# New engine orders for a blocked attention kernel, with two first products split by columns and a last part in two

## The chip, the cores and the metric

The kernel runs on one core of a Trainium2 chip. The metric is the device time of one execution in microseconds (us). Most executions of a kernel agree within 0.3%.

## The reference

One layer of multi-head attention with a cached K and V: B = 8 batches, SQ = 112 queries, D = 640 model width, H = 32 heads of DH = 192, SK = 512 keys. All tensors are bf16.

```
q = (x @ wq).reshape(B, Sq, H, Dh).transpose(0, 2, 1, 3)
scores = einsum("bhqd,bhkd->bhqk", q, k_cache) * (Dh ** -0.5)
p = softmax(scores, axis=-1)
o = einsum("bhqk,bhkd->bhqd", p, v_cache)
out = o.transpose(0, 2, 1, 3).reshape(B, Sq, H * Dh) @ wo
```

## The kernel before

**Tiles and stages.** The 32 heads are taken in four rounds of eight. A round has two groups (batches 0 to 3, 4 to 7), so there are eight groups g, and 64 steps n: a step is one batch and half a round, four heads. An operation below is named as in the kernel's lists: a kind, then its numbers.

- ("XT", c): five transposes on PE of 128 rows of x (L656); ("evX", c) copies them from PSUM into xT_sb (the copy helper, L146 on ACT, L147 on DVE).
- ("Q", g, lp, c): a tile of q for group g, pair of heads lp and 128 of its 384 columns c, five matmuls of 128x448 (L721); ("evQ", ...) copies it into qr, and ("qc", n) on POOL, or DVE, brings the second parts of step n's heads together in qh (L762, L763).
- ("KT", i, p): 24 transposes of K for the few K tiles that are loaded as they lie (L673); most K tiles are transposed by the DMA that loads them (("K", i), L158). A K tile serves two steps, 2i and 2i+1.
- ("Sm", n, j) and ("St", n, j): the scores of step n (L774). ("smax", n, k) on DVE takes the maximum and copies the scores to s_sb (L831), ("exp", n, k) on ACT (L836), ("rc", n, j) the reciprocal of the sums (L848), ("norm", n, k) the scaling of p on DVE (L840).
- ("PT", n): 32 transposes of p on PE (L875) with two copies ("evPT", n, t); for steps 57 to 61 instead ("TD", n), a transposing DMA (L859).
- ("PVt", n), ("PVm", n, t): p @ v (L907, L919), copied by ("evPV", n).
- ("O", g, m, half): o @ wo for block m of 128 output columns (L941); ("oacc", g, m) adds it up on DVE (L955, L956). For the last group the part of batch 6 is ("O6", ...) with ("oacc6", ...) (L974, L984), and that of batch 7 ("OL", s, part) with ("oaccL", part) (L998, L1007, L1011). ("OF", b) transposes the sum of batch b back (L1023), ("oout", b) copies it into xT_sb, and ("OUT", b) stores it (L646).

**What sets the order.** Nothing is scheduled while the kernel runs. Five lists written out by hand, ORDER_PE, ORDER_ACT, ORDER_DVE, ORDER_POOL and ORDER_SP, give each engine its operations in order; a copy or small operation runs on the engine in whose list it stands. BANKS gives each PSUM tile one of eight banks; a tile waits until the copy that reads the tile before it in its bank is done. The class Plan numbers the semaphores from the lists, and each engine waits for an operation's inputs just before it issues it, so an engine that waits holds all that stands behind in its list.

**Loads.** All transfers stand on SP, in order. A load waits for its place: K i for the last St of step 2(i−4)+1, which frees the slot; a V half (L167) for the p @ v of the step three tiles before; and each load waits for the landing of an earlier one, so that about 0.95 tile sizes are under way (AHEAD, L1107). The TD of a step waits for its norm operations. SP being in order, a held load holds all later ones, the OUT transfers too.

**Buffers that couple steps.** s_sb has three places, so a smax waits for the exp three before it. The exp operations of step n wait until p of step n − 2 is transposed (its PT, or the landing of its TD), as p_sb is used anew.

**Head and tail.** PE begins with 18 matmuls on zeros (idle, L690), until x has landed; the zeros are set by DVE (L1142). In the tail, batch 7's last products have two parts: part 0 has the blocks 0, 1 and 4, part 1 the blocks 2 and 3. Part 0 is summed by two DVE operations (L1007 for the blocks 0 and 1, L1011 for 4), part 1 by one; ("OF", 7) needs both.

## Time and profile before

| what | value |
|---|---|
| three runs | 434.97, 433.34, 434.41 us; median 434.41 |
| the profiled execution | 434.01 us, of which 432.2 span |
| instructions in the span | 16330 |
| DMA over the span | 122.05 MB moved, mean 282 GB/s |
| granted TensorE clock | 1.00 |

The span is what the profile covers, from the first instruction to the last; the 1.8 us around it are the start and end of the execution. In a timeline row stand the start in us, the length, the engine (PE the matmuls, PEld its weight loads, SPq the issuing of DMAs), the line of the kernel, the operation, output<-input by name, shapes and count; in brackets the idle time before it and what ended that. Names of tiles are those of the place in memory: places are used anew, so K or p can stand under accT, wo_sb or wq_sb. In the rows of the chain of waits stand the start, the length and the work that the end of the execution hung on. A row of groups has the busy time, the mean length in ns, and the idle time before.

### The profile page before, as it was taken

To read this page: it belongs to the slowest core of one execution; us is meant where nothing else is said; L and a number is where in the kernel's file an instruction comes from. 1 tells how busy PE (TensorE), PEld (TensorE's weight loads), DVE (VectorE), ACT (ScalarE), POOL (GpSimd) and SP (SyncE) were. 2 spreads that over 40 slices of the span, in tenths; PEclk is the share of its full clock that TensorE was granted. 3 is DMA by queue.
4 is the path that set the end of the run, shared out by engine and by line. 5 is a ranking of instruction groups with operands and counts; after the bars stand their busy time and mean duration, and the time that the engine had idled before them with its cause. 6 is when DMAs were issued, how large, how long until landed. Compare 5 with 4: busy or idle time off the path is not lost.

```text
span 432.2 us, 16330 instructions
## 1 busy us (share of the span) xinstructions
PE 419.0 (97%) x6805; PEld 289.5 (67%) x6805; DVE 345.6 (80%) x1087; ACT 335.9 (78%) x734; POOL 88.7 (21%) x124
## 2 busy tenths in 40 slices
PE   7999997999999999999999999999999999999986
PEld 4556665676766667677766666766667667666886
DVE  2689887889788888888798997869888679987871
ACT  3489998988868686889777858978778787766763
POOL 0102222122212222222122212222222120212100
PEclk9999999999999999999999999999999999999999
DMA  8999999999999999999999999999999999999772
GB/s 273 372 334 366 346 289 238 330 331 187 238 355 239 215 342 372 321 255 353 269 235 345 277 238 331 369 333 225 236 274 250 216 289 360 314 224 256 197 216 84
DMA packets 218923, 122.05 MB, mean 282 GB/s; under 512 B 165216, under 2 KB 218848, under 8 KB 218848
## 3 DMA queue, kind: packets, MB, share of 16 engines
q1 hardware_dynamic: 218848, 120.99, 107.5%
q8 instruction: 54, 0.88, 0.9%
q14 instruction: 21, 0.17, 0.1%
HBM read 78.22 MB, written 1.15 MB: 184 GB/s over the span
## 4 chain that ended last, share of the span: by engine, by line
PE 84%; DMA 7%; DVE 6%; ACT 1%; issue 1%; SPq 0%; DVEq 0%; ACTq 0%
PE ps L721 20%; PE ps L774 18%; PE ps L941 17%; PE ps L919 12%; PE ps L907 7%; PE ps L875 7%; DMA wq_sb<-p_sb 3%; DVE s_sb L831 3%; PE ps L673 2%; DVE p_sb L840 2%; DMA vt<-in_v_cache_dram 2%; DMA accT<-in_k_cache_dram 1%; DMA kt<-in_x_dram 1%; PE ps L974 1%; ACT p_sb L836 1%
## 5 line engine op out<-in xcount | busy, mean ns | idle before, releaser
L836 ACT ACTIVATE p_sb<-s_sb,nmx 112x512 bf16<-112x512 f32 x256 | 182.8, 718 | 34.0 <-DVE s_sb L831 28.5
L831 DVE TENSOR_SCALAR_CACHE_REDUCE s_sb<-ps 112x512 f32<-112x512 f32 x256 | 169.3, 683 | 30.5 <-PE ps L774 22.1
L762 POOL COPY qh<-qr 64x672 bf16<-64x672 bf16 x59 | 44.0, 746 | 309.1 <-PE ps L774 266.0
L721 PE MATMUL ps<-xT_sb,wq_sb 128*128 128x448 bf16 x480 | 101.5, 353 | 2.4 <-DVE kt L147 1.6
L774 PE MATMUL ps<-kt,qr 128*128 128x256 bf16 (+1 forms) x512 | 95.3, 272 | 0.9 <-DVE s_sb L831 0.7
L941 PE MATMUL ps<-oT_sb,wo_sb 128*128 128x448 bf16 (+1 forms) x480 | 91.4, 341 | 0.0
L840 DVE TENSOR_SCALAR p_sb<-p_sb,rinv 112x512 bf16<-112x512 bf16 x256 | 88.1, 373 | 0.8
L774 PE MATMUL ps<-kt,qh 128*128 128x256 bf16 (+1 forms) x512 | 87.8, 272 | 0.0
L941 PEld LDWEIGHTS ps<-oT_sb,wo_sb 128*128 128x128 bf16 x480 | 44.7, 98 | 36.0 <-issue 0.4
L721 PEld LDWEIGHTS ps<-xT_sb,wq_sb 128*128 128x128 bf16 x480 | 42.6, 98 | 39.0 <-issue 3.5
L146 ACT ACTIVATE oT_sb<-ps 128x672 bf16<-128x672 f32 x64 | 46.5, 726 | 24.8 <-PE ps L919 24.3
L146 ACT ACTIVATE pT_sb<-ps 128x1024 bf16<-128x1024 bf16 (+1 forms) x61 | 55.9, 923 | 10.7 <-PE ps L875 10.7
L774 PEld LDWEIGHTS ps<-kt,qr 128*128 128x128 bf16 (+1 forms) x512 | 44.1, 96 | 22.1 <-issue 12.9
L919 PE MATMUL ps<-pT_sb,vt 128*128 128x112 bf16 x944 | 55.2, 213 | 0.0
L919 PEld LDWEIGHTS ps<-pT_sb,vt 128*128 128x128 bf16 x944 | 47.5, 98 | 4.0
L836 ACT ACTIVATION_READ_ACCUMULATOR p_sb<-s_sb,nmx 112x1 f32 x256 | 49.6, 194 | 0.0
L774 PEld LDWEIGHTS ps<-kt,qh 128*128 128x128 bf16 (+1 forms) x512 | 44.1, 96 | 6.0
L763 POOL COPY qh<-qr 64x672 bf16<-64x672 bf16 x59 | 44.0, 745 | 2.5
L146 ACT ACTIVATE qr<-ps 128x448 bf16<-128x448 f32 x58 | 31.2, 541 | 13.0 <-PE ps L721 12.9
L147 DVE COPY pT_sb<-ps 128x768 bf16<-128x768 bf16 (+1 forms) x57 | 34.5, 607 | 6.9 <-PE ps L875 6.8
L875 PE MATMUL ps<-ident,p_sb 64*128 64x64 bf16 (+1 forms) x1888 | 37.1, 185 | 1.5 <-issue 0.6
L875 PEld LDWEIGHTS ps<-ident,p_sb 64*128 64x128 bf16 (+1 forms) x1888 | 33.4, 94 | 7.1 <-issue 3.1
(58 smaller groups left out, 269.0 us busy)
## 6 DMA issues: line engine op xcount, KB each, us to landing
vt<-in_v_cache_dram SPq DMA_DIRECT2D x64, 768.0 KB, 6.7
wo_sb<-in_wo_dram SPq DMA_DIRECT2D x8, 960.0 KB, 7.6
wq_sb<-in_wq_dram SPq DMA_DIRECT2D x7, 960.0 KB, 7.5
wo_sb<-in_k_cache_dram SPq DMA_DIRECT2D x6, 768.0 KB, 7.3
accT<-in_k_cache_dram SPq DMA_DIRECT2D x4, 768.0 KB, 6.4
vt<-in_k_cache_dram SPq DMA_DIRECT2D x2, 768.0 KB, 8.2
kt<-in_k_cache_dram SPq DMA_DIRECT2D x2, 768.0 KB, 6.9
out_dram<-xT_sb SPq DMA_DIRECT2D x8, 140.0 KB, 2.2
```

The costliest lines, as they stand in the source:

```text
L146: return e.activation(dst, src, ACTF.Copy)
L147: return e.tensor_copy(dst, src)
L721: mm = e.matmul(ps[:, bank, 0:SG], w, v, start=(dc == 0), stop=(dc == DC - 1))
L762: e.tensor_copy(dst[64:128, :, 0:3, :], src[0:64])
L763: return e.tensor_copy(dst[0:64, :, 1:4, :], src[64:128])
L774: return e.matmul(ps[:, 2 * j + odd, hs], q, ktb[j][lo:hi, :, blk, h * 128:(h + 1) * 128], start=first, stop=last, skip_group_check=True)
L831: return e.tensor_scalar(s_sb[:, a, :].rearrange("p (e c) -> p e c", e=2), ps[0:SQ, 2 * j:2 * j + 2, h * 256:(h + 1) * 256], -scale, None, ...
L836: return e.activation(p_sb[:, k, :], s_sb[:, a, :], ACTF.Exp, bias=nmx[:, k:k + 1], scale=-1.0, accum_out=rsum[:, k:k + 1])
L840: return e.tensor_scalar(p_sb[:, k, :], p_sb[:, k, :], rinv[:, k:k + 1], None, op0=ALU.mult)
L875: ends.append(e.transpose(psb[:, bank + t, i * w:(i + 1) * w], p_sb[lo:hi, (4 * n + k) % 8, q * 128:(q + 1) * 128], ident[lo:hi, lo:hi]))
L919: mm = e.matmul(ps[:, b0 + j, 2 * h * SQ:(2 * h + 1) * SQ], vtb[:, h0 + 2 * j + h, d0:d0 + 128], pT(j, h, q), start=(q == 0), stop=(q == 3))
L941: mm = e.matmul(ps[:, bank_of["O", g, m], 0:nc_], wo_sb[:, k, m * 128:(m + 1) * 128], oT_sb[:, g % 2, k, 0:nc_], start=(k == 0), stop=(k = ...
```

## The change

ORDER_PE, ORDER_ACT, ORDER_DVE, ORDER_POOL and BANKS are written anew. ORDER_SP stays as it is. PE's list goes from 736 to 739 operations, ACT's from 476 to 463 and DVE's from 819 to 833: 74 copies go from ACT to DVE, 58 from DVE to ACT, and four operations are new. Beside the lists:

- The two first products ("Q", 0, 1, 1) and ("Q", 0, 1, 0) are split by columns: a new operation ("Qa", ...) computes the columns 0 to 256, which need the first two copies of x alone, and "Q" the other 192.
- The two last parts hold the blocks 0, 1, 2 and 3, 4. Part 0 is summed by one DVE operation of three blocks, and the final transposes, the copy and only then the store of batch 7 are in two parts as well, ("OF", 7, part) and ("oout", 7, part). The copies of batch 6 and of part 1 of batch 7 go to DVE.
- The matmuls on zeros at the start are 8 of 512 columns instead of 18 of 256.

```diff
+    FIRST = ((0, 1, 1), (0, 1, 0))
+    XA = 256
...
-        zeros = k3_flat[:, 4 * D:4 * D + 256]
+        zeros = k3_flat[:, 4 * D:4 * D + 512]
...
         ORDER_PE = [
-            ('XT', 0), ('XT', 1), ('XT', 3), ('XT', 2), ('Q', 0, 1, 1), ('Q', 0, 0, 0), ('Q', 0, 0, 1), ('Q', 0, 1, 0),
+            ('XT', 0), ('XT', 1), ('XT', 3), ('XT', 2), ('Qa', 0, 1, 1), ('Qa', 0, 1, 0), ('Q', 0, 1, 1), ('Q', 0, 1, 0),
...
-            ('PVt', 7), ('PVm', 7, 0), ('PVm', 7, 1), ('Sm', 11, 0), ('Sm', 11, 1), ('St', 11, 0), ('St', 11, 1), ('PT', 9),
+            ('PVt', 7), ('PVm', 7, 0), ('PVm', 7, 1), ('Sm', 11, 0), ('Sm', 11, 1), ('PT', 9), ('Q', 2, 3, 2),
+            ('St', 11, 0), ('St', 11, 1), ('PVt', 8), ('PVt', 9), ('PVm', 9, 0), ('PVm', 9, 1), ('PVm', 8, 0),
...
-            add("SP", ("OUT", b), [("oout", b)], emit, f"mOUT{b % DC}", 16)
+            add("SP", ("OUT", b), [("oout", b)] if b < B - 1 else [("oout", b, 0), ("oout", b, 1)], emit, f"mOUT{b % DC}", 16)
...
-                mm = e.matmul(ps[:, 5, 0:256], zeros[:, 0:128], zeros, start=True, stop=True)
+                mm = e.matmul(ps[:, 5, :], zeros[:, 0:128], zeros, start=True, stop=True)
...
-            def emit(e):
+            def emit(e, c0, c1):
                 for dc in range(DC):
                     w, v = q_tile(g, lp, c, dc, 0, 128)
-                    mm = e.matmul(ps[:, bank, 0:SG], w, v, start=(dc == 0), stop=(dc == DC - 1))
+                    mm = e.matmul(ps[:, bank, c0:c1], w, v[:, c0:c1], start=(dc == 0), stop=(dc == DC - 1))
                 return mm
-            add("PE", ("Q", g, lp, c), q_need(g, lp), emit)
+            if (g, lp, c) in FIRST:
+                add("PE", ("Qa", g, lp, c), [wq_piece[0, lp], ("evX", 0), ("evX", 1)], lambda e: emit(e, 0, XA))
+            add("PE", ("Q", g, lp, c), q_need(g, lp), lambda e: emit(e, XA if (g, lp, c) in FIRST else 0, SG))
...
-        LAST = {0: (7, 0), 1: (7, 1), 4: (7, 2), 2: (6, 0), 3: (6, 1)}
+        LAST = {0: (7, 0), 1: (7, 1), 2: (7, 2), 3: (6, 0), 4: (6, 1)}
+        ENDS = [(0, 1, 2), (3, 4)]
...
-            blocks = (0, 1, 4) if part == 0 else (2, 3)
...
+                m0, n = ENDS[part][0], len(ENDS[part])
+                return e.tensor_tensor(oF[:, 1, m0:m0 + n, 3 * SQ:SG, 0],
+                                       ps[:, 7 - part, 0:n * SQ].rearrange("p (c s) -> p c s", c=n),
+                                       accT[:, 1, m0:m0 + n, 3 * SQ:SG], op=ALU.add)
...
+        def o_final(b, *part):
+            bank = bank_of["OF", b, *part]
+            blocks = ENDS[part[0]] if part else tuple(range(DC))
+            cols = slice(blocks[0] * 128, blocks[-1] * 128 + 128)
...
+            need = ([("oaccL", *part)] if part else [("oacc6", g) for g in range(3)] if b == B - 2 else
...
-            idle(e, 18)
+            idle(e, 8)
```

**PE at its start.** The rows give the line, the operation, output<-input, the shape that is streamed, and the count. In the kernel before, PE runs the matmuls on zeros, the transposes of x, four whole products and the first K transposes:

```order
L690 MATMUL ps<-kt 128x256 x18
L656 MATMUL ps<-ident,kt 128x128 x20
L721 MATMUL ps<-xT_sb,wq_sb 128x448 x20
L673 MATMUL ps<-ident,vt 128x64 x48
L721 MATMUL ps<-xT_sb,wq_sb 128x448 x5
```

In the changed kernel (lines are two further on) the same place reads:

```order
L692 MATMUL ps<-kt 128x512 x8
L658 MATMUL ps<-ident,kt 128x128 x20
L723 MATMUL ps<-xT_sb,wq_sb 128x256 x10
L723 MATMUL ps<-xT_sb,wq_sb 128x192 x10
L723 MATMUL ps<-xT_sb,wq_sb 128x448 x10
L675 MATMUL ps<-ident,vt 128x64 x48
L723 MATMUL ps<-xT_sb,wq_sb 128x448 x10
L658 MATMUL ps<-ident,accT 128x128 x15
```

Two of the four products are now ten matmuls of 256 and ten of 192 columns, and the remaining transposes of x stand together.

**DVE at the softmax of step 59.** In the kernel before, DVE has three maxima of step 59, two sums of output blocks (L956), the fourth maximum, then reciprocals and scalings of step 59 among maxima of step 60:

```order
L831 TENSOR_SCALAR s_sb,nmx<-ps 112x512 x3
L956 TENSOR_TENSOR accT<-ps,accT 128x448 x2
L831 TENSOR_SCALAR s_sb,nmx<-ps 112x512
L848 RECIPROCAL rinv<-rsum 112x2
L840 TENSOR_SCALAR p_sb<-p_sb,rinv 112x512
L831 TENSOR_SCALAR s_sb,nmx<-ps 112x512
L848 RECIPROCAL rinv<-rsum 112x2
L831 TENSOR_SCALAR s_sb,nmx<-ps 112x512
L840 TENSOR_SCALAR p_sb<-p_sb,rinv 112x512 x3
```

In the changed kernel (lines four further on):

```order
L835 TENSOR_SCALAR s_sb,nmx<-ps 112x512 x4
L852 RECIPROCAL rinv<-rsum 112x2
L960 TENSOR_TENSOR accT<-ps,accT 128x448
L844 TENSOR_SCALAR p_sb<-p_sb,rinv 112x512
L960 TENSOR_TENSOR accT<-ps,accT 128x448
L852 RECIPROCAL rinv<-rsum 112x2
L844 TENSOR_SCALAR p_sb<-p_sb,rinv 112x512 x2
L835 TENSOR_SCALAR s_sb,nmx<-ps 112x512 x2
L844 TENSOR_SCALAR p_sb<-p_sb,rinv 112x512
```

The two sums stand behind the fourth maximum, and two maxima of step 60 instead of one stand between the second reciprocal and the last scaling of step 59.

**DVE at its end.** The last rows of DVE's order before, with the copies of p, the sums of batch 6 (L984) and those of batch 7:

```order
L147 COPY pT_sb<-ps 128x16x48
L984 TENSOR_TENSOR accT<-ps,accT 128x112
L147 COPY pT_sb<-ps 128x16x48
L984 TENSOR_TENSOR accT<-ps,accT 128x2x112
L1007 TENSOR_TENSOR accT<-ps,accT 128x2x112
L1011 TENSOR_TENSOR accT<-ps,accT 128x112
L1007 TENSOR_TENSOR accT<-ps,accT 128x2x112
```

And of the changed kernel:

```order
L149 COPY pT_sb<-ps 128x16x64 x2
L988 TENSOR_TENSOR accT<-ps,accT 128x2x112 x2
L1009 TENSOR_TENSOR accT<-ps,accT 128x3x112
L1009 TENSOR_TENSOR accT<-ps,accT 128x2x112
L149 COPY xT_sb<-ps 112x640
L149 COPY xT_sb<-ps 112x256
```

One sum of three blocks stands for two, and the copies of batch 6 and of the last two blocks of batch 7 are DVE's.

More of the change, by code (lines that the diff above doesn't have):

```diff
@@ L995, in emit @@
                     w, o = wo_k(k, 3)
-                    for m in blocks:
+                    for m in ENDS[part]:
                         bank, c = LAST[m]
@@ L1069, in build_mha_kernel @@
         o_last_acc(1)
-        for b in range(B):
+        for b in range(B - 1):
             o_final(b)
+        o_final(B - 1, 0)
+        o_final(B - 1, 1)
         def tiles(op):
```

502 lines of the change are left out of this document (254 added, 248 removed), and 247 rows, old and new, of tables (BANKS, ORDER_PE, ORDER_POOL).

## The prediction

> **What bounds the kernel now.** I began with the page: busy time, the DMA share in 40 slices, and the chain that ended last.
>
> ```profile
> PE 419.0 (97%) x6805; PEld 289.5 (67%) x6805; DVE 345.6 (80%) x1087; ACT 335.9 (78%) x734; POOL 88.7 (21%) x124
> DMA  8999999999999999999999999999999999999772
> PE 84%; DMA 7%; DVE 6%; ACT 1%; issue 1%; SPq 0%; DVEq 0%; ACTq 0%
> ```
>
> Two resources are full almost to the end, PE and the DMA engines. The new lists hold the same products, so PE's work stays; what can move is PE's waiting, 432.2 − 419.0 = 13 us, and the start of loads. Next come windows (stretch, length, then busy time and count on PE, PEld, DVE, ACT, POOL, clock, DMA share, GB/s) and the timeline rows in which PE waits.
>
> ```profile
> 160.00:200.00 40.00, 39.86 (x692) 27.42 (x691) 35.18 (x109) 31.96 (x69) 9.07 (x13) 1.00 1.11 321
> 67.50:73.60 6.10, 6.08 (x126) 4.30 (x126) 4.37 (x15) 4.39 (x9) 0.19 (x2) 1.00 1.23 263
> 74.20:420.10 345.90, 343.92 (x5428) 237.91 (x5428) 289.48 (x920) 274.11 (x611) 76.98 (x104) 1.00 1.12 282
> ```
>
> ```profile
> 22.05 0.87 PE L673 MATMUL ps<-ident,wo_sb 64*128 64x64 bf16 x48 [0.47 <-DMA wo_sb<-in_k_cache_dram]
> 30.54 0.87 PE L673 MATMUL ps<-ident,accT 64*128 64x64 bf16 x48 [0.44 <-DMA accT<-in_k_cache_dram]
> 67.52 2.05 PE L721 MATMUL ps<-xT_sb,wq_sb 128*128 128x448 bf16 x10 [1.56 <-DVE kt L147]
> 74.24 0.45 PE L875 MATMUL ps<-ident,p_sb 64*128 64x64 bf16 x20 [0.64 <-issue]
> 421.30 0.36 PE L974 MATMUL ps<-oT_sb,wo_sb 128*128 128x112 bf16 x4 [1.09 <-issue]
> ```
>
> From 74.2 to 420.1 PE idles 2.0 us: nothing that an order saves there is large. Before it stand two waits for K landings and two that I read as waits for PE's own program: 67.52 and 74.24 lie 126 + 126 matmuls and weight loads apart, with four waits 256 instructions, and from 74.24 to the third such wait (1.09 us at 421.30) stand 10856, with the waits 43 times 256. DVE is named at 67.52, but its copy was long done.
>
> The third look was SP's queue: which waits hold loads, and the long rows.
>
> ```profile
> SPq L46 <- PE ps L774: 1.6, 1, 1.6
> SPq L167 <- PE ps L919: 1.8, 2, 1.2
> 92.36 24.52 SPq L158 DMA_TRANSPOSE kt<-in_k_cache_dram  x3
> 371.68 14.10 SPq L158 DMA_TRANSPOSE kt<-in_k_cache_dram  x2
> 385.88 5.08 SPq L859 DMA_TRANSPOSE wq_sb<-p_sb  x2
> ```
>
> The first two, three waits of 3.4 us together, are the loads that visibly wait for PE: K 7 (for scores, 1.6) and V 6,0 and V 6,1 (for values, 1.8). The last two rows show the tail's gate: K 31 holds SP until 371.68 + 14.10 = 385.78, and the transposing load of step 57 follows at 385.88. The tail starts when the stream of loads lets it, not when PE is ready; a gain on PE must first become a gain of the stream.
>
> **The change, part by part.** The sum is against this execution, 434.01 us (span 432.2 and 1.8 around it), 0.4 under the median 434.41.
>
> *Head.* Rows of the first 10 us:
>
> ```profile
> 0.86 0.17 DVE L1142 MEMSET kt<- 128x128 uint32 x1
> 1.09 4.02 PE L690 MATMUL ps<-kt 128*128 128x256 bf16 x18 [1.09 <-DVE kt L1142]
> 5.81 1.49 PE L656 MATMUL ps<-ident,kt 128*128 128x128 bf16 x20 [0.70 <-DMA kt<-in_x_dram]
> 6.28 1.30 ACT L146 ACTIVATE xT_sb<-ps 128x640 bf16<-128x640 bf16 x2 [4.06 <-PE ps L656]
> 7.05 0.89 DVE L147 COPY xT_sb<-ps 128x640 bf16<-128x640 bf16 x2 [5.27 <-PE ps L656]
> 8.08 3.94 PE L721 MATMUL ps<-xT_sb,wq_sb 128*128 128x448 bf16 x20 [0.79 <-DVE xT_sb L147]
> 14.20 0.49 DVE L147 COPY xT_sb<-ps 128x640 bf16<-128x640 bf16 x1 [2.46 <-PE ps L656]
> ```
>
> Before, the first product waits for all four copies of x, to 8.08; twenty matmuls of 448 columns take 3.94, about 0.19 each. The first ten would now be ten of 256 columns (0.19 × 256/448 = 0.108, together 1.1) after two copies, from about 7.1 to 8.2, and ten of 192 (0.081, 0.8) after the other two, near 8.4 to 9.25. Before, these ten ended at 8.08 + 1.9 = 9.98: 0.7 gained. This is then caught by the landings behind the waits at 22.05 and 30.54. By the lists and these durations 23.4 instead of 22.2 us of PE work stand ahead of the product that needs the second landing, so up to 1.1 us ahead survive; bounds 0.3 and 1.1, and I take **0.8**. The warm-up is 8 × 512 = 4096 instead of 18 × 256 = 4608 columns on a memset twice as long (0.17 more at most): both end before the landing at 5.7 that starts the transposes, so I put it at nothing; without that cover, 0.2.
>
> [...]
>
> *Code waits.* If the program comes in pieces of 256, a piece must be worked in no less time than the next needs to arrive. With the traced durations in the new order the piece before the first wait still has 5.0 us of work, so 1.56 stays; the next has 7.9 instead of 5.8, so 0.64 should go; the one after has 5.0 instead of 6.8 and may wait anew, between 0 and 1.8 (taken: 0.2); the last one keeps 4.4, and 1.09 stays. PE is then 0.8 + 0.6 − 0.2 = 1.2 ahead near 85 us; bounds 0 and 2.5.
>
> [...]
>
> *The stream.* V 6,0 and V 6,1 start earlier by up to those 1.2. Against it stands K 9: its slot is freed by the second half of step 11's scores, and the change puts the transposes of step 9 and a first product ahead of that half.
>
> ```profile
> 91.84 0.27 PE L774 MATMUL ps<-kt,qr 64*128 64x256 bf16 x1
> 91.95 0.63 PE L875 MATMUL ps<-ident,p_sb 64*128 64x64 bf16 x32
> 92.51 1.12 PE L721 MATMUL ps<-xT_sb,wq_sb 128*128 128x448 bf16 x5
> ```
>
> The scores end at 92.11 and K 9 is issued at 92.36: at most 0.25 of slack. The two put ahead take 0.56 (91.95 to 92.51) and 5 × 0.19 = 0.95, 1.5 us. With PE 1.2 ahead K 9 comes 0.3 − 0.25, about 0.05 late. The train behind it takes 8.2 a load against 7.05 in the pair at 371.68, a sign of backlog, so a few tenths may vanish or be won. At TD 57 I take **−0.4**; bounds −1.2 and +1.25 (nothing gained on PE, nothing absorbed).
>
> *Copies, banks, POOL.* 74 copies go from ACT to DVE and 58 back, and tiles change banks. In 160 to 200 DVE is busy 35.2 and ACT 32.0 of 40: PE, busy for 39.86 of them, covers it. Uncovered, one copy late costs 0.5 (row at 14.20), one of the swapped pairs on POOL twice 0.75:
>
> ```profile
> L762 POOL COPY qh<-qr 64x672 bf16<-64x672 bf16 x59 | 44.0, 746 | 309.1 <-PE ps L774 266.0
> ```
>
> POOL is busy 9 of the 40 and waits for PE, not PE for it. Taken as nothing, bounds one copy either way, ±0.5.
>
> *Tail, softmax of step 59.* Rows of the chain of waits (start, length, what):
>
> ```profile
> 390.18 1.24 DVE L956 TENSOR_TENSOR accT<-ps,accT 128x448 bf16<-128x448 f32 x2
> 392.23 0.71 DVE s_sb L831 x2
> 394.85 0.60 DVE s_sb L831 x2
> 395.45 1.05 DVE p_sb L840 x3
> 396.52 6.12 DMA wq_sb<-p_sb
> 402.69 0.58 PE ps L907 x16
> 411.10 1.71 SPq L646 DMA_DIRECT2D out_dram<-xT_sb  x2
> ```
>
> Two sums of 0.62 stood at 390.18 in DVE's idle time and now stand behind the last maximum of step 59 (ends 392.94), and two maxima of step 60 (0.60 each) stand ahead of the last scaling. From 392.93: reciprocal 0.2, sum 0.62, scaling 0.35, sum 0.62, reciprocal 0.1, two scalings 0.7, two maxima 1.2, scaling 0.35, giving 397.07 for 396.50: TD 59, its values at 402.69, and all behind them come **0.55** later (bounds 0 and 0.7, since PE runs without a gap from 402.69 to 420.2). OUT 2's copy now stands behind step 63's first scores, some 0.4 past 411.10, and V 31 queues behind it on SP; its values are needed only behind 421.30, so I put this at 0 (bounds 0 and 0.4). One final transpose stands ahead of the code wait: **−0.1**.
>
> *Last part in two.*
>
> ```profile
> 427.21 0.41 DVE accT L1007
> 427.62 0.17 DVE accT L1011
> 427.80 0.42 DVE accT L1007
> 428.26 0.51 PE ps L1023 x5
> 428.79 0.70 ACT xT_sb L146
> ```
>
> The last copy ends at 429.49. Now the three-block sum is one op (between 0.41 and 0.41 + 0.17; 0.55, to 427.76), its transposes and ACT copy (0.6 of 0.70) run beside the two-block sum (to 428.2), and two transposes (0.51 less three of at most 0.075, from 1.49 for 20: 0.3) and, after one whole copy on DVE (0.49, to 428.7), a copy of 256 columns (0.3) follow: end near 429.0, **−0.5** (bounds 0 and −0.8).
>
> **Sum:** −0.4 + 0.55 − 0.1 − 0.5 = −0.45: 434.01 − 0.45, about **433.6**; its own range 432.2 to 434.9, half of each bound above taken together.
>
> **The rivals.** *B, the code waits go in full.* PE has three more list items and other waits, so every piece ends elsewhere. Without 1.56 and 0.64 PE is 3.0 ahead, and the stream takes the 1.8 for which V 6,0 and V 6,1 waited. Of the 1.09 at 421.30 I count 0.5, since V 31's landing is next. −1.8 − 0.5 − 0.1 + 0.55 − 0.5 = −2.35: **431.7**. For: the pieces are reshuffled. Against: the first has as little work as before.
>
> *C, slower: K 9.* If PE has no lead at 92 us (the change does nothing for the head, its gain caught at 30.5, or a new code wait eats it), K 9 waits 1.5 − 0.25 = 1.25 for the moved scores, and the loads behind it reach TD 57 so much later: 1.25 + 0.55 − 0.1 − 0.5 = +1.2, **435.2**; with a new code wait like the 1.56 on top, 436.8. It costs from a lead under 1.25 on. For: the loads behind K 9 are issued back to back. Against: their backlog.
>
> [...]
>
> *E, the copies at the end.* ACT now has the output copy of batch 5 between the two last value copies, and it waits for an earlier output's landing:
>
> ```profile
> 426.54 0.70 ACT L146 ACTIVATE xT_sb<-ps 112x640 bf16<-112x640 bf16 x1 [1.24 <-DMA out_dram<-xT_sb]
> ```
>
> If that still lands at 426.5, the value copy behind it ends near 427.9 and the last products follow, 2 late: **435.5**. Against: the outputs it waits for are now issued earlier.
>
> **How the numbers follow.** Within 0.5% (2.2 us) is what a measurement of this kernel can't tell from no change. Forecast 0.45 (0.08 faster by more, 0.35 within, 0.02 slower), B 0.25 (0.20, 0.05, 0), C 0.15 (0, 0.09, 0.06), D 0.07 (0, 0.06, 0.01), E 0.08 (0, 0.03, 0.05): faster 0.28, same 0.58, slower 0.14. The range reaches from B's far side (all of the 1.09 and a little of K 7's 1.6), 430.9, to between C's two times, 436.0.
>
> **What would show it.** Head: ten 256-column matmuls from 7.1, products ending 0.7 earlier, shorter waits after 30.5. Code: waits without releaser at about 67, none near 74, one near 420. Stream: K 9's issue against 92.36, TD 57's against 385.88. Tail: 0.55 more from TD 57 to TD 59, last copy about 0.5 nearer to the last product. The prediction is wrong if TD 57 moves by over 1.3 either way, or if new waits stand on PE between 100 and 385.

## The result and the profile after

The changed kernel is slower: 439.90 us (median of 4 runs, 439.29 to 442.02) beside 433.88 (4 runs, 432.69 to 434.97) of the kernel before on the same chip. The ratio is 1.0124, interval 1.0081 to 1.0166. The profiled execution is 442.02 us, its span 440.2; before it was 434.01 and 432.2. So the trace has 8.0 us to account for, the medians 6.0. Executions that ran slower throughout (up to 443.0 us for before) are left out of all ratios, though not of the medians in the table below. Two lines of its page:

```profile
PE 420.5 (96%) x6805; PEld 288.6 (66%) x6805; DVE 354.8 (81%) x1100; ACT 324.9 (74%) x721; POOL 88.8 (20%) x124
PE 76%; DVE 10%; DMA 8%; ACT 3%; issue 2%; SPq 0%; DVEq 0%; ACTq 0%
```

PE's work is what it was (420.5 for 419.0). Its idle time grew from 13 to 440.2 − 420.5 = 20 us, and DVE's share of the chain of waits from 6 to 10%. Where the idle time lies is seen in the windows (stretch, length, busy time and count on PE, PEld, DVE, ACT, POOL, clock, DMA share, GB/s), first of before, then of the changed kernel:

```profile
40.00:80.00 40.00, 37.02 (x802) 25.64 (x800) 33.41 (x107) 37.31 (x82) 8.91 (x12) 1.00 1.10 297
120.00:360.00 240.00, 239.48 (x3718) 162.60 (x3715) 200.41 (x633) 189.16 (x418) 56.70 (x76) 1.00 1.14 289
```

```profile
40.00:80.00 40.00, 35.39 (x766) 24.53 (x765) 35.56 (x109) 32.20 (x71) 10.54 (x14) 1.00 1.10 298
120.00:360.00 240.00, 238.34 (x3712) 161.02 (x3708) 203.36 (x631) 182.83 (x410) 58.30 (x78) 1.00 1.15 282
160.00:200.00 40.00, 39.14 (x624) 26.05 (x622) 34.54 (x103) 29.70 (x66) 9.05 (x12) 1.00 1.11 318
74.20:420.10 345.90, 338.41 (x5272) 231.06 (x5265) 292.39 (x914) 260.83 (x591) 77.75 (x104) 1.00 1.12 276
```

In 40 to 80 PE's idle time goes from 2.98 to 4.61 us, DVE works 2.15 more and ACT 5.1 less. From 120 to 360 PE idles 1.66 for 0.52, and in 160 to 200, the window that the prediction argued from, 0.86 for 0.14. The last row, beside the 2.0 us of before, holds 7.5 us of idle time: part of it is the tail, whose waits now fall inside the window.

The rows of PE in the changed kernel, from the first product to 85 us, that are begun after a wait or answer to the prediction:

```profile
7.39 2.82 PE L723 MATMUL ps<-xT_sb,wq_sb 128*128 128x256 bf16 x23
15.77 0.27 PE L778 MATMUL ps<-kt,qr 128*128 128x256 bf16 x1 [0.59 <-DVE qh L767]
18.21 0.52 PE L675 MATMUL ps<-ident,vt 64*128 64x64 bf16 x24 [0.87 <-DMA vt<-in_k_cache_dram]
32.53 0.87 PE L675 MATMUL ps<-ident,accT 64*128 64x64 bf16 x48 [0.62 <-DMA accT<-in_k_cache_dram]
55.49 0.93 PE L723 MATMUL ps<-xT_sb,wq_sb 128*128 128x448 bf16 x4 [0.70 <-issue]
61.26 0.53 PE L675 MATMUL ps<-ident,accT 64*128 64x64 bf16 x24 [0.19 <-ACT qr L148]
63.11 0.68 PE L675 MATMUL ps<-ident,accT 64*128 64x64 bf16 x33 [0.47 <-issue]
64.49 0.62 PE L879 MATMUL ps<-ident,p_sb 64*128 64x64 bf16 x32 [0.70 <-DVE p_sb L844]
70.01 3.00 PE L723 MATMUL ps<-xT_sb,wq_sb 128*128 128x448 bf16 x15 [1.17 <-DVE p_sb L844]
80.00 0.52 PE L675 MATMUL ps<-ident,wo_sb 64*128 64x64 bf16 x24 [0.92 <-DVE s_sb L835]
```

The products of q begin at 7.39 instead of 8.08, as wanted, and step 0's scores 1.4 earlier, behind a wait for a copy (15.77). Then PE waits for the landings at 18.21 and 32.53. The wait of before at 74.24 is gone, the one at 67.52 stands at 70.01, and two without a releaser are new (55.49, 63.11). At 61.26, 64.49 and 80.00 PE waits for a copy of q, a scaling of p and a maximum, 1.8 us together; before had one such wait of 0.35 in this stretch. The second trace of the changed kernel has these three at the same places with 0.18, 0.70 and 0.92, so they belong to the order. It has neither the two waits for landings nor the one at 55.49, and 0.29 at 63.11: those are not in every execution.

SP's queue, first the groups of waits for PE that the prediction named (total, times, longest; the first row is before over the whole execution, the next two are the changed kernel), then the changed kernel's timeline at K 9, at K 31 and step 57's transposing load, and at step 59's and 60's:

```profile
SPq L167 <- PE ps L919: 2.4, 4, 1.2
SPq L169 <- PE ps L923: 10.3, 9, 2.6
SPq L46 <- PE ps L778: 5.6, 3, 2.7
96.97 14.67 SPq L160 DMA_TRANSPOSE kt<-in_k_cache_dram  x2
377.90 15.46 SPq L160 DMA_TRANSPOSE kt<-in_k_cache_dram  x2
393.47 4.35 SPq L863 DMA_TRANSPOSE wq_sb<-p_sb  x2
404.73 6.76 SPq L863 DMA_TRANSPOSE wq_sb<-p_sb  x2
```

Twelve waits of 15.9 us instead of five of 4.0 (K 7's 1.6 with the first row). The view names what came last by the profile, so some of this can be landings. With the end of everything that the lists make a load wait for set beside its issue, PE held loads for 13.1 us in this trace and for 3.3 in that of before: loads that before waited only for their turn now wait for PE. K 9 is issued at 96.97 instead of 92.36, and step 57's load at 393.47 instead of 385.88. That is 7.59 of the 8.0 us, before the tail has begun. The tail adds the rest, by the chain's piece for step 57's load, DVE's timeline behind its landing (its first row, L831, is the first maximum of step 60 before), and PE's rows that waited there:

```profile
393.47 4.97 DMA wq_sb<-p_sb
```

```profile
394.08 0.69 DVE L831 TENSOR_SCALAR_CACHE_REDUCE s_sb<-ps 112x512 f32<-112x512 f32 x1 [0.59 <-PE ps L774]
399.36 0.69 DVE L835 TENSOR_SCALAR_CACHE_REDUCE s_sb<-ps 112x512 f32<-112x512 f32 x1 [2.84 <-ACT p_sb L840]
400.15 0.64 DVE L960 TENSOR_TENSOR accT<-ps,accT 128x448 bf16<-128x448 f32 x1
400.94 0.67 DVE L960 TENSOR_TENSOR accT<-ps,accT 128x448 bf16<-128x448 f32 x1
401.57 1.55 DVE L844 TENSOR_SCALAR p_sb<-p_sb,rinv 112x512 bf16<-112x512 bf16 x2
403.03 0.68 DVE L835 TENSOR_SCALAR_CACHE_REDUCE s_sb<-ps 112x512 f32<-112x512 f32 x1
404.25 0.45 DVE L844 TENSOR_SCALAR p_sb<-p_sb,rinv 112x512 bf16<-112x512 bf16 x1
400.12 0.28 PE L778 MATMUL ps<-kt,qr 128*128 128x256 bf16 x1 [1.35 <-DVE s_sb L835]
406.44 0.28 PE L778 MATMUL ps<-kt,qr 128*128 128x256 bf16 x1 [1.05 <-DVE s_sb L835]
411.88 0.58 PE L911 MATMUL ps<-wq_sb,vt 128*64 128x112 bf16 x16 [1.18 <-DVE accT L960]
```

From the landing at 398.44, DVE takes the last maximum of step 59 (399.36), then the two sums, and the first maximum of step 60 begins only at 403.03, 4.6 behind the landing. Before it was 394.08 − 391.30 = 2.8. The two PE waits at 406.44 and 411.88 are new; the second trace of the changed kernel has them with 1.06 and 1.17.

### The profile page after: what moved, and what is told of

It reads as the page before. It is cut to its first block, busy times and chain, and to the rows that moved or that the text cites. A ratio compares the mean times of both kernels' runs of the same rounds, so it can differ in the third digit from the quotient of the medians.

```text
span 440.2 us, 16299 instructions
## 1 busy us (share of the span) xinstructions
PE 420.5 (96%) x6805; PEld 288.6 (66%) x6805; DVE 354.8 (81%) x1100; ACT 324.9 (74%) x721; POOL 88.8 (20%) x124
## 3 DMA queue, kind: packets, MB, share of 16 engines
HBM read 78.22 MB, written 1.15 MB: 180 GB/s over the span
## 4 chain that ended last, share of the span: by engine, by line
PE 76%; DVE 10%; DMA 8%; ACT 3%; issue 2%; SPq 0%; DVEq 0%; ACTq 0%
PE ps L778 17%; PE ps L945 16%; PE ps L723 16%; PE ps L923 10%; PE ps L911 6%; PE ps L879 6%; DVE s_sb L835 5%; DVE p_sb L844 2%; ACT p_sb L840 2%; DMA vt<-in_k_cache_dram 2%; DMA accT<-in_k_cache_dram 2%; PE ps L675 2%; DMA wq_sb<-in_wq_dram 1%; DMA vt<-in_v_cache_dram 1%; DMA wq_sb<-p_sb 1%
## 5 line engine op out<-in xcount | busy, mean ns | idle before, releaser
L723 PE MATMUL ps<-xT_sb,wq_sb 128*128 128x448 bf16 (+2 forms) x490 | 101.4, 349 | 1.9 <-DVE p_sb L844 1.2
L778 PE MATMUL ps<-kt,qr 128*128 128x256 bf16 (+1 forms) x512 | 96.4, 272 | 3.6 <-DVE s_sb L835 2.4
L945 PE MATMUL ps<-oT_sb,wo_sb 128*128 128x448 bf16 (+1 forms) x480 | 92.9, 341 | 0.3 <-DVE kt L149 0.2
L723 PEld LDWEIGHTS ps<-xT_sb,wq_sb 128*128 128x128 bf16 x490 | 43.8, 98 | 39.7 <-issue 3.6
L149 DVE COPY pT_sb<-ps 128x1024 bf16<-128x1024 bf16 (+1 forms) x71 | 43.5, 623 | 8.3 <-PE ps L879 8.1
L148 ACT ACTIVATE pT_sb<-ps 128x768 bf16<-128x768 bf16 (+1 forms) x47 | 41.9, 894 | 9.9 <-PE ps L879 9.7
L840 ACT ACTIVATION_READ_ACCUMULATOR p_sb<-s_sb,nmx 112x1 f32 x256 | 48.5, 190 | 0.0
L148 ACT ACTIVATE qr<-ps 128x448 bf16<-128x448 f32 x63 | 32.7, 535 | 13.4 <-PE ps L723 13.0
L879 PE MATMUL ps<-ident,p_sb 48*128 48x48 bf16 (+1 forms) x1888 | 37.1, 185 | 1.8 <-DVE p_sb L844 1.1
L879 PEld LDWEIGHTS ps<-ident,p_sb 48*128 48x128 bf16 (+1 forms) x1888 | 33.1, 94 | 8.3 <-issue 2.8
```

The lines of the kernel that those rows point to most:

```text
L148: return e.activation(dst, src, ACTF.Copy)
L149: return e.tensor_copy(dst, src)
L723: mm = e.matmul(ps[:, bank, c0:c1], w, v[:, c0:c1], start=(dc == 0), stop=(dc == DC - 1))
L778: return e.matmul(ps[:, 2 * j + odd, hs], q, ktb[j][lo:hi, :, blk, h * 128:(h + 1) * 128], start=first, stop=last, skip_group_check=True)
L840: return e.activation(p_sb[:, k, :], s_sb[:, a, :], ACTF.Exp, bias=nmx[:, k:k + 1], scale=-1.0, accum_out=rsum[:, k:k + 1])
L879: ends.append(e.transpose(psb[:, bank + t, i * w:(i + 1) * w], p_sb[lo:hi, (4 * n + k) % 8, q * 128:(q + 1) * 128], ident[lo:hi, lo:hi]))
```

## The experiments

The five lists and the banks can be cut at a step: up to the scores of step n they follow one kernel, from there the other. So the change was taken apart into five stretches: steps 0 to 3 with the split products and the new first matmuls, steps 4 to 13, steps 14 to 58, the tail's order, and the last part in two. The table has all kernels run, o for the lists of before and n for the new ones, with the median, the ratio to the runs of before on the same chip, and two readings of their one trace each: by how much the first scores of step 10 began later than in the trace of before, and when step 57's load landed.

| kernel | 0–3 | 4–13 | 14–58 | tail | last | median us | ratio [95%] | step 10 | landing |
|---|---|---|---|---|---|---|---|---|---|
| before | o | o | o | o | o | 433.88 | | | 391.30 |
| before, again | o | o | o | o | o | 434.66 | 0.998 [0.995, 1.002] | +0.7 | 391.21 |
| new steps 0–3 | n | o | o | o | o | 435.54 | 1.000 [0.998, 1.002] | −0.3 | 393.77 |
| last part in two | o | o | o | o | n | 435.84 | 1.003 [1.000, 1.007] | +0.1 | 391.33 |
| new tail order | o | o | o | n | o | 436.78 | 1.004 [1.000, 1.007] | +0.8 | 391.64 |
| new tail | o | o | o | n | n | 437.81 | 1.008 [1.004, 1.013] | +0.4 | 394.77 |
| new head | n | n | o | o | o | 435.43 | 1.004 [1.000, 1.007] | +2.2 | 392.97 |
| new steps 4–13 | o | n | o | o | o | 437.90 | 1.007 [1.004, 1.010] | +2.4 | 395.38 |
| old steps 14–58 | n | n | o | n | n | 438.95 | 1.008 [1.005, 1.012] | +1.6 | 395.71 |
| old head | o | o | n | n | n | 438.67 | 1.011 [1.007, 1.015] | +0.7 | 392.66 |
| old steps 4–13 | n | o | n | n | n | 439.06 | 1.010 [1.007, 1.014] | −0.3 | 392.82 |
| new steps 14–58 | o | o | n | o | o | 441.80 | 1.015 [1.009, 1.021] | +1.7 | 398.01 |
| old tail | n | n | n | o | o | 441.45 | 1.016 [1.011, 1.020] | +3.4 | 398.52 |
| changed | n | n | n | n | n | 439.90 | 1.012 [1.008, 1.017] | +3.3 | 398.44 |
| changed, again | n | n | n | n | n | 440.13 | 1.013 [1.008, 1.019] | +2.1 | 397.64 |
| changed, St 11 back | n | n | n | n | n | 440.64 | 1.012 [1.006, 1.018] | +3.6 | 400.10 |
| changed, sums back | n | n | n | n | n | 442.65 | 1.017 [1.013, 1.020] | +3.1 | 400.62 |

**The changed kernel again, and its halves.** No edit in the first; the others are cut at step 14 or step 59.

```diff
 ORDER_PE, ORDER_ACT, ORDER_DVE, ORDER_POOL, BANKS
-new throughout
+new head: new up to ("Sm", 14, 0), from there old
+old head: old up to ("Sm", 14, 0), from there new
+new tail: old up to ("Sm", 59, 0), from there new, with the last part in two
```

> The changed kernel itself, for a second trace of it. If its loss is in its orders, the stretches that lost time in the first trace lose it again: step 57's transposing load some 5 to 7 us later than before, and PE waits again near 55, 63, 70 and 80 us. If the two slow stretches of the loads without any wait for PE (the head to 30 us, the K tiles 24 and 30) were that execution's alone, they are not there again, and step 57's load comes 4 us later or less. Time 439 to 442 us.

> The changed orders up to step 13's scores (with the two split products and the new warm-up), then the orders, banks and last part of before. Theory 1 (the early order makes PE late where the loads wait for it, and the stream keeps that): most of the 6 us, 437.5 to 440. Theory 2 (the later orders hold loads between 100 and 385 us): 433 to 435.5. Theory 3 (the tail): 434 or less.

> The reverse: the orders of before up to step 13's scores, with whole first products and the old warm-up, then the changed orders and the changed last part. Theory 1: 433 to 435.5. Theory 2: 437.5 to 440. Theory 3: as the changed kernel, 439 to 441.

> The orders of before up to step 58, then the changed tail with the last part in two. By the terms of the prediction the tail alone is about +0.55 - 0.1 - 0.5, nothing: 433.5 to 434.5. If the tail is where the time is lost (theory 3): 438 to 440.

Measured: 440.13, 435.43, 438.67 and 437.81 us. No half is faster than before. By its median no half has the whole loss, but the interval of the old head (1.007 to 1.015) reaches the whole's ratio. With the new head step 10 begins 2.2 us late, with the old one 0.7 and 0.4. These times are those of theory 2: the new head comes out in its 433 to 435.5 and the old head, with everything later new, in its 437.5 to 440. The tail alone lies between the two ranges given for it.

**Before again, the tail in parts, K 9.** The second puts the last part in two into the lists of before, the third the new tail's order without it. The fourth is the changed kernel with the second half of step 11's scores ahead of what the change had put before it.

```diff
 ORDER_PE (last part in two)
-("OF", 7)
+("OF", 7, 0), ("OF", 7, 1)
 ORDER_PE (St 11 back)
-("Sm", 11, 1), ("PT", 9), ("Q", 2, 3, 2), ("St", 11, 0), ("St", 11, 1)
+("Sm", 11, 1), ("St", 11, 0), ("St", 11, 1), ("PT", 9), ("Q", 2, 3, 2)
```

> The kernel before itself, for a second trace and many times. In c4 the orders are those of before up to step 58, and yet step 57's transposing load came 3.9 us later than in the first trace of before. If that is the chance of one execution, this trace too has its trains of K loads elsewhere by 1 to 3 us, and its times scatter over 432 to 440 as before. If the loads of a given program are steady, step 57's load is within 0.5 of 385.9 again, and the ratio is 1.000 within 0.003.

> The orders of before, with only the last part in two (blocks 0, 1, 2 and 3, 4; the copies of batch 6 and of the second part on DVE). The prediction's term: -0.5 (bounds 0 and -0.8), 433.5 to 434.5. If the last part is what costs 3 us in c4: 437 to 438.

> The orders of before up to step 58, then the changed orders with the last part as before. The prediction's terms: +0.55 - 0.1, 434.5 to 435.5. If the order of the tail costs the 3 us of c4: 437 to 438.

> The changed kernel with the second half of step 11's scores put back ahead of step 9's transposes and the first product. If K 9's wait (1.3 and 2.5 us in the two traces) reaches the end: 1.3 to 2 us less than the changed kernel, 438 to 438.5. If the train of K loads behind it absorbs it, as K 8's landing (0.6 to 1.0 late) suggests: 439.5 to 440.5, no change.

Measured: 434.66, 435.84, 436.78 and 440.64 us. The second and third lie between the two ranges given for each. Putting step 11's scores back brings nothing that the runs can tell: 1.0120 beside the changed kernel's 1.0124 and 1.0133, with an interval of ±0.6% (2.7 us), wider than the 1.3 to 2 us at stake; its traced execution also had a stretch at a granted clock of 0.61 (last section). K 9 does come 4.6 us later in the changed kernel, held by those scores, but the first load behind the train of K loads is issued 1.9 later, at 118.81 for 116.93; in the second traces of the two kernels it even comes 0.25 earlier (117.54 for 117.79), though K 9 is 2.4 late there. The last part in two makes no difference that the runs can tell in the old lists.

**The head in two, and the tail's sums.** The head is cut once more, at step 4. In the last kernel the two sums stand ahead of step 59's last maximum again, as in before.

```diff
 ORDER_*, BANKS (new steps 0-3)
+new up to ("Sm", 4, 0), from there old
 ORDER_*, BANKS (new steps 4-13)
+old up to ("Sm", 4, 0), new up to ("Sm", 14, 0), from there old
 ORDER_DVE (sums back)
-("smax", 59, 3), ("rc", 59, 0), ("oacc", 6, 3), ("norm", 59, 1), ("oacc", 6, 1)
+("oacc", 6, 3), ("oacc", 6, 1), ("smax", 59, 3), ("rc", 59, 0), ("norm", 59, 1)
-("smax", 60, 0), ("smax", 60, 1), ("norm", 59, 3)
+("norm", 59, 3), ("smax", 60, 0), ("smax", 60, 1)
```

("oacc", 6, 4) also moved up there, ahead of ("smax", 61, 0).

> The changed orders up to step 3's scores (with the split products and the new warm-up), then everything of before. Theory 4 (the loss of the head is PE waiting for copies, scalings and maxima between 60 and 80 us): PE reaches step 10's scores within 0.8 us of before (84.2; the other traces of the old head lie at +0.1 to +0.8), time 434 to 435.5. Rival (the loss comes from the first 45 us: loads, clock, split products): step 10's scores 2 to 3.5 late, as in the four traces of the new head, time 435.5 to 437.

> The reverse: the orders of before up to step 3, the changed ones for steps 4 to 13, then those of before; whole first products, old warm-up. Theory 4: PE waits near 61 (0.5), 64 (0.5 to 0.9), 72 (0.4) and 79 us (1.1) for DVE and ACT, reaches step 10's scores 2 to 3.5 late, and stays so to step 57; time 435.5 to 437. Rival: step 10 within 0.8, time 434 to 435.5.

> The changed kernel with four DVE operations of the tail put back: the two sums of step 59's place ahead of the last maximum, the last scaling of step 59 ahead of the maxima of step 60, and the sum of block 4 ahead of the maxima of step 61. Theory 5 (the tail's loss is PE waiting for DVE in steps 60 to 62: 1.05 at the second scores of step 61, 1.17 at the values of step 59): these two waits shrink to under 0.5 together, the store of the last batch comes 38 instead of 39.2 us after step 57's load has landed, time 1 to 2 less than the changed kernel, 438 to 439. Rival (the transposing loads of steps 59 and 60 set the tail whatever DVE does): 39 us and more from that landing, 439.5 to 440.5.

Measured: 435.54, 437.90 and 442.65 us. Steps 0 to 3 lose nothing (1.000), so the head's loss is in steps 4 to 13. The second lies above theory 4's 437 and the third above both its ranges. The window 40 to 80 of the two, new steps 0 to 3 first:

```profile
40.00:80.00 40.00, 36.63 (x780) 25.40 (x778) 33.75 (x107) 35.84 (x80) 10.24 (x15) 1.00 1.10 298
```

```profile
40.00:80.00 40.00, 34.88 (x786) 24.43 (x781) 34.76 (x105) 32.80 (x72) 9.06 (x12) 1.00 1.11 276
```

PE idles 1.75 us more with the new steps 4 to 13, but nearly all of it, 1.72, is in the first two rows below (PE's timeline, new steps 4 to 13). They stand at the joint, where the new lists take over, and neither whole kernel nor the new head has them. The other two are the changed kernel's own, at 64.49 and 80.00 there:

```profile
46.63 0.53 PE L691 MATMUL ps<-ident,wo_sb 64*128 64x64 bf16 x24 [0.61 <-issue]
49.15 2.07 PE L739 MATMUL ps<-xT_sb,wq_sb 128*128 128x448 bf16 x10 [1.11 <-DVE kt L147]
63.28 0.62 PE L893 MATMUL ps<-ident,p_sb 64*128 64x64 bf16 x32 [0.34 <-DVE p_sb L858]
79.13 0.52 PE L691 MATMUL ps<-ident,wo_sb 64*128 64x64 bf16 x24 [0.92 <-DVE s_sb L849]
```

So this run alone makes the stretch look dearer than it is. The new head has the same steps without that joint: it is 2.2 us late at step 10, and its ratio is 1.004.

The last wait, at 79.13, comes about thus. The transposes ("KT", 5, 0) use a bank that a maximum of step 8 must free. Before, PE did not wait there: between step 8's scores and the transposes PE had ("PT", 6) and two products:

```diff
 ORDER_PE
-("St", 8, 1), ("PT", 6), ("Q", 2, 2, 0), ("Q", 2, 0, 1), ("KT", 5, 0)
+("St", 8, 1), ("Q", 2, 2, 0), ("PT", 6), ("KT", 5, 2), ("KT", 5, 0)
```

A product (1.0 us) went to an earlier place and half a microsecond of transposes came for it, while ("smax", 8, 1) went behind ("smax", 8, 2).

The sums did not repair the tail. The two waits that they were blamed for did shrink, from 1.05 to 0.31 us and from 1.18 to none, but the time is no less: theory 5 has the waits right and the time wrong. Its trace can't say why, for it has a wait of its own. DVE's timeline of that kernel, whose step 57 landed at 400.62, then a row of PE and a window with the granted clock:

```profile
402.08 1.20 DVE L978 TENSOR_TENSOR accT<-ps,accT 128x448 bf16<-128x448 f32 x2 [0.72 <-PE ps L963]
403.18 0.67 DVE L853 TENSOR_SCALAR_CACHE_REDUCE s_sb<-ps 112x512 f32<-112x512 f32 x1
386.23 0.76 PE L941 MATMUL ps<-pT_sb,vt 128*128 128x112 bf16 x12 [1.79 <-issue]
387.30:390.70 3.40, 3.40 (x31) 2.29 (x26) 0.52 (x3) 1.97 (x5) 0.00 (x0) 0.51 1.07 186
```

The maximum begins 2.56 us behind the landing instead of 0.93, because the sums ahead of it wait for their blocks. PE made these late after a wait of 1.79 us and 3.4 us at a granted clock of 0.51; in the changed kernel's own trace they were ready 1.2 us before the landing. Whether the sums would hold the maximum up in an execution without that wait is not shown.

**The middle alone, and one stretch undone at a time.** The first kernel has the new steps 14 to 58 in the lists of before. The other three take one stretch out of the changed kernel.

```diff
 ORDER_*, BANKS
+new steps 14-58: old up to ("Sm", 14, 0), new up to ("Sm", 59, 0), from there old
+old steps 14-58: new up to ("Sm", 14, 0), old up to ("Sm", 59, 0), from there new
+old steps 4-13: new up to ("Sm", 4, 0), old up to ("Sm", 14, 0), from there new
+old tail: new up to ("Sm", 59, 0), from there old, with the old last part
```

> The orders of before up to step 13 and in the tail from step 59 on, the changed ones between; whole first products, old warm-up and last part. By the differences of the runs so far (c3 less c4 and d3) the middle costs 1 to 2 us: PE waits 0.4 each near 174, 225 and 302 us, 0.8 more in all than before, and is 1 to 1.5 late at step 58; time 435.5 to 437. If the middle is free and the parts of the loss are the steps 4 to 13 and the tail alone: step 58 within 0.5 of where PE stands at step 14, time 434.5 to 435.5.

> The changed kernel with the lists and banks of before from step 14's scores to step 59's; head and tail are the changed kernel's. Theory A (the losses of the three stretches add, and the middle holds the largest, 2 to 4 us): about 437 (436 to 438), step 57's load within 4 us of before. Rival (the middle adds only the 1.1 us of its visible PE waits): 438.5 to 439.5. Rival (what counts is that PE is 2 to 3 us behind when it enters step 14, and the middle carries it through whatever its order): 439.5 to 441, no gain. Sizes from the traces: PE idles 0.9 us from step 14 to 58 with the old order and 2.0 with the new one.

> The changed kernel with the lists and banks of before from step 4's scores to step 14's. Theory A (losses add; steps 4 to 13 hold 1 to 2.5 us by the runs that had them alone): 437.5 to 439; PE within 1 us of before at step 14 where the changed kernel is 2 to 3 behind. Rival (the loads give it back later in any case): no gain, 439.5 to 441.

> The changed kernel up to step 59's scores, with the lists and banks of before from there and the old last part. Theory A (the tail's order costs 1.0 to 1.7 us between step 57's landing and the last stores, the last part in two next to nothing): 438 to 439, step 60's load issued about 9 us behind step 57's landing instead of 11.6. Rival (the late stream alone sets the end; the tail is the same either way): 439.5 to 441. It says also whether the seam of the earlier run with new steps 14 to 58 (a wait for a sum of batch 6 of 2.2 us at step 59) was that run's own.

Measured: 441.80, 438.95, 439.06 and 441.45 us. The first is above both ranges given for it, the second in that of its first rival, the third at the edge of theory A's, and the fourth above both. Undoing the middle gives back 0.45% (1.0126, the mean of the changed kernel, its repeat and the one with St 11 back, less 1.0081), 2.0 us; this is at the edge of its interval of ±0.45%. Undoing steps 4 to 13 gives 0.25%, 1.1 us, inside an interval of ±0.47%, and undoing the tail nothing. The tail can't be judged that way: both kernels with the new middle and the old tail stop at step 59, one for 2.24 us, the other for 2.25 (PE's timeline of the first, new steps 14 to 58):

```profile
392.87 2.44 PE L960 MATMUL ps<-oT_sb,wo_sb 128*128 128x448 bf16 x12 [2.24 <-DVE rinv L867]
```

The new middle leaves output blocks of group 6 for later, and the old tail takes them in another order, so PE waits 2.2 us for a bank that the sum ("oacc", 6, 2) frees; neither whole kernel has this wait. These two medians are too high by some of that. The other joint costs less: the three kernels with the new tail behind the old middle wait 0.82 us at step 59, which neither whole kernel does.

**What follows from the table.** The landing of step 57's load, averaged over the traces of each kind, with the lowest and the highest:

| steps 4–13 | steps 14–58 | traces | mean landing | lowest to highest |
|---|---|---|---|---|
| o | o | 6 | 392.3 | 391.2 to 394.8 |
| n | o | 3 | 394.7 | 393.0 to 395.7 |
| o | n | 3 | 394.5 | 392.7 to 398.0 |
| n | n | 5 | 399.1 | 397.6 to 400.6 |

So the two stretches together delay the stream by some 7 us on average, and no landing of the last row is as early as any of the first. Each alone does so by some 2 us on average, but these ranges overlap with the first row's, and the two highest landings of the last row are those of traces with a stretch at a low granted clock (0.61 and 0.51). That the two together cost more than their sum is not shown: the times give 0.7% and 1.5% for each alone, the second with a wait of its own at the joint, and 1.6% for both together.

Each stretch can also be timed by itself in all seventeen traces. From the first scores of step 4 to those of step 10 it takes 39.0 to 40.9 us in the nine with old steps 4 to 13 and 40.4 to 42.5 in the eight with new ones, on average 1.5 more (1.3 without the one that has a stretch at 0.61 of the clock there). From the first scores of step 14 to the landing it takes 283.4 to 287.3 us in the nine with the old middle and 284.9 to 289.7 in the eight with the new one, on average 2.8 more (2.5 without the one that has a stretch at 0.51).

From that landing to the issue of the last store it takes 38.1 us with the old tail and last part (5 traces of before or with a new head) and 38.9 with the new ones (7 traces, without the kernel of the sums): 0.8 more. Steps 0 to 3 cost and bring nothing.

Steps 4 to 13 act on the stream through PE. When a load's issue is set beside the end of the last thing it waits for, PE held loads after 110 us for 0.4 to 5.4 us in all eight kernels with new steps 4 to 13, and for 0.06 or less in all nine with the old ones. This does not go with the size of the delay: the kernel with the sums back held loads for 0.4 us and landed last. So a path through PE is shown, but not how much of the delay takes it.

How the middle delays the stream stays open. Where it stood behind old steps 4 to 13 (three kernels), PE held loads for no more than 0.06 us after 110 us. PE's idle time from step 14 to 58 is 2.0, 4.0 and 2.4 us there, but with the old middle it is anything from 0.9 to 3.6, so idle time does not tell the two apart. Not separated either are PE's new order, the moved copies and the new banks: each list was only run with the others of its kind.

## Why the prediction was wrong

The forecast was 433.6 us, in a range of 430.9 to 436.0; the kernel takes 439.9, and none of the rivals reached it. By its steps:

- **Head, 0.8 us ahead: wrong in effect.** The product's start came as worked out (7.39 for 8.08), and step 0's scores began 1.4 us earlier. The two landings took it back: PE waits 0.87 and 0.62 us for them, and step 1 begins 0.7 later than before. The second trace, with a slow start (last section), has no such wait, and the kernel with nothing but this part new has the ratio 1.000. The bound of 0.3 from below was too high.
- **Code waits: half right.** 1.56 stayed (1.17 at 70.01) and 0.64 went. But the stretches of PE's list ahead of these were not looked at: 0.70 and 0.47 are new at 55.49 and 63.11. That makes 0.1 us more than before up to 75 us in this pair of traces, where 0.4 less was expected. But the waits differ between executions of one kernel: the second trace of before has 0.57, 1.56 and 0.64 there and 0.35 instead of 1.09 in the tail, that of the changed kernel 0.31, 0.29 and 1.17. So neither that 0.1 nor the 0.23 that stood in for the 1.09 late in the tail (430.00, below) can be put down to the new order. That all these are waits for the program is a reading of counts, and no view names it: from 55.49 to 63.11 PE has 125 matmuls and 126 weight loads, from there to 70.01 126 of each, as from 67.52 to 74.24 before.
- **Copies, banks, POOL, taken as nothing with ±0.5: this step failed first.** It argued from the window 160 to 200, where PE is busy for 39.86 of 40 us and DVE for 35.2. In steps 4 to 13, where K is still transposed on PE and its banks change owners with the scores', three waits for copies, scalings and maxima make 1.8 us, and over all traces steps 4 to 9 take some 1.5 us longer, where nothing ±0.5 was the forecast. PE is 3.3 us behind at step 10 instead of 1.2 ahead: 1.4 of it stood at step 4 already, behind the waits for landings, and 1.9 came from there on. The second trace, without those landings, is 2.1 behind. (By the lists 71 copies go from ACT to DVE, not 74: 476 − 71 + 58 = 463; six operations are new and two are gone.)
- **The stream, −0.4 with bounds of −1.2 and +1.25: the largest error.** It is +7.6 in the trace. The sign followed from PE's: its bound took a PE without any gain as the worst case, and PE was behind. The middle, which the prediction put among the copies that PE covers, delays the stream by some 2 us too, by the averages of the landings; what in the middle does it is not known.
- **K 9: right that the wait appears, wrong that it costs.** It is issued 4.6 us late, of which 3.1 come with V 6,1 ahead of it; the train behind absorbs much of it (the first load behind it is 1.9 late), and taking the cause away gains nothing that the run can tell. So the price of rival C was not seen, though a run with an interval of 2.7 us can't rule 1.25 out. Its clause "the change does nothing for the head" held all the same.
- **Tail, +0.55 at step 59: right in kind, short by a term.** TD 59 is issued 6.29 us behind step 57's landing instead of 5.22, 1.07 more. Step 60 was left out of the sum: behind the same sums and scalings its first maximum is 1.8 later, its load is issued 11.5 instead of 9.1 us behind the landing, and PE waits for two maxima and a sum (rows at 400.12, 406.44, 411.88). In all the new tail is 0.8 us longer in the traces; by the ratios in the lists of before 1.5 (old last part) and 3.5 (new one), of which 0.82 is the wait at the joint, and in the second a landing that came 3.5 later than before's.
- **Last part in two, −0.5: right for the copies, not for the end.** From the last product's end to the last copy's end it took 427.76 to 429.49, 1.73 us. After (timeline of the changed kernel):

```profile
430.00 0.22 PE L978 MATMUL ps<-oT_sb,wo_sb 128*128 128x112 bf16 x1 [0.23 <-issue]
432.93 3.11 PE L1001 MATMUL ps<-oT_sb,wo_sb 128*128 128x112 bf16 x60
435.49 1.00 DVE L1009 TENSOR_TENSOR accT<-ps,accT 128x336 bf16<-128x336 f32 x2 [4.51 <-PE ps L1001]
436.38 0.81 DVE L149 COPY xT_sb<-ps 112x640 bf16<-112x640 bf16 x2
436.53 0.49 ACT L148 ACTIVATE xT_sb<-ps 112x384 bf16<-112x384 bf16 x1 [2.52 <-PE ps L1023]
```

  The copies end at 437.19, 1.15 us after the last product's end at 436.04: 0.58 gained. But SP is then still at work on the store of batch 6. The issue of the last store ends 1.93 us behind the last product (437.97) where it ended 2.08 behind before (429.84), and the span ends only 0.3 nearer to that product. So the term was 0.2 to 0.3, not 0.5: it left out SP's queue. Alone in the old lists the part can't be seen (435.84 us, 1.003).
- **Rivals B and E** did not come: waits that were read as waits for code remain (0.70, 0.47 and 1.17), and the outputs' copies don't hold the end. **D** stands among the chances with 0.07, but no run shows that the first matmuls set how fast PE starts. What they show is a slow start in five of the seventeen traces, of either kind: 2.19 to 2.29 us for the transposes of x instead of 1.5 (last section). One such trace has lost the delay by step 10 (+0.1), another has not (+1.7).

What the prediction named as proof against itself was the right test: step 57's load moved by over 1.3 us, and new waits stand on PE between 100 and 385. What is shown, then, is where the time went: to the order of steps 4 to 13, through PE's waits for copies, scalings and maxima, and to the stream of loads. Not shown is the mechanism by which the middle, and the two stretches together, cost the stream its 7 us.

## What to carry to other kernels

Where two resources are both full, "the engine is covered" must be checked where its cover is thinnest: here in ten steps, not in the window in the middle where PE is busy for 39.86 of 40 us. A new order is judged by the waits for bank and copy in each stretch, one by one, because loads in an ordered queue can begin to wait for a PE that is late (here it held them for 13.1 us instead of 3.3). A list cut at a step and joined to the old one tells stretches apart, but the joint can have a wait of its own (0.8 to 2.2 us here), so each stretch is put in alone and also taken out of the whole, and the traces are looked through for waits that neither whole kernel has.

## What the runs showed of the hardware

- **PE ran at a granted clock of 0.50 to 0.61 behind three waits of 1.79 to 2.41 us, and at its usual pace behind others as long.** In the kernel with St 11 back PE waited 1.98 us without a releaser, and the ten products behind it took 3.35 us where they take 2.06 elsewhere. PE's timeline, then the window with the granted clock:

```profile
49.53 0.22 PE L897 MATMUL ps<-ident,p_sb 64*128 64x64 bf16 x4 [1.98 <-issue]
49.69 3.35 PE L741 MATMUL ps<-xT_sb,wq_sb 128*128 128x448 bf16 x10
```

```profile
49.50:53.00 3.50, 3.47 (x16) 1.32 (x17) 2.30 (x7) 2.16 (x4) 0.00 (x0) 0.61 0.70 192
```

  The granted clock is 0.61 in these 3.5 us, 0.82 from 53 to 55 and 1.00 from 55 on. Two more of the seventeen traces have such a stretch, of some 3.4 us: behind 1.79 us in the kernel with the sums back (clock 0.51, shown there) and behind 2.41 us at 396.46 in the one with the new tail (0.50; its mean over that execution is 0.995). Other waits were as long, and the products behind them went at their usual pace: behind 1.85 us (new head, at 49.73) ten took 2.06 us, and behind 2.24 and 2.25 us at step 59 (old tail) twelve took 2.44, where the next twelve of the second of these traces take 2.43 (at 399.03). What decides between the two is not shown.
- **The slow start varies by execution.** The twenty transposes of x took 2.29 instead of 1.5 us with the new first matmuls and with the old ones (the changed kernel again):

```profile
6.10 2.29 PE L658 MATMUL ps<-ident,kt 128*128 128x128 bf16 x20 [1.29 <-DMA kt<-in_x_dram]
```

  It was so in five of the seventeen traces (2.29 us in four, 2.19 for nineteen of the transposes in one), three of nine with the new first matmuls and two of eight with the old; the second trace of before lies between, with 1.88. So few traces show no sign that the matmuls ahead decide it. The kernel with the last part in two is 1.4 us late at step 0 for it and within 0.1 of before at step 10; the one with new steps 14 to 58 is still 1.7 late there.
- **The stream of loads drifts by itself.** With the same order up to step 58, step 57's load landed between 391.2 and 394.8 us in five traces. The executions of the kernel before that are counted in the ratios took from 430.4 to 437.6 us, so they agree within 1.7%, not within the 0.3% stated ahead of the prediction. Each stretch's share is therefore known to about 2 us only. That the whole loses some 5 us is not in doubt: by the intervals of the changed kernel and its repeat it is 3.4 to 8.1.
